# The state matmuls of a linear attention: two heads per matmul, attached to the bursts of the local attention

## Chip, cores, metric

One core of a Trainium2 chip. The metric is device microseconds (us) of one execution. A "drain" below is the time, some 0.1 us, that TensorE loses where the tile size of its matmuls changes.

## The reference, cut to what matters

Two attentions over the same `x` (2048 tokens, 1024 columns, 32 heads of 32) are mixed by a gate. Branch A is linear: a state `kv` (32 x 32 per head) and `z` are summed over all tokens. Branch B is local: every token looks at 8 keys, two apart.

```python
def _A_ref(x, wqkv, wo):
    q, k, v = ...                                   # [B, 32 heads, S, 32]
    phi = lambda t: jnp.where(t > 0, t + 1, jnp.exp(t)) + 1e-6
    pq, pk = phi(q), phi(k)
    kv = jnp.einsum("bhsd,bhse->bhde", pk, v)       # the state
    z = jnp.einsum("bhsd->bhd", pk)
    o = jnp.einsum("bhqd,bhde->bhqe", pq, kv) / (jnp.einsum("bhqd,bhd->bhq", pq, z)[..., None] + 1e-6)
    return o... @ wo
def _B_ref(x, wqkv, wo):
    ...                                             # scores over 8 keys two apart, softmax, times v, @ wo
g = _sigmoid((x * gate_w).sum(-1, keepdims=True))
return g * a + (1 - g) * b
```

## The kernel before

The kernel is written as a list of operations; a planner in it then orders each engine's instructions by costs, dependencies and priorities (`P.op`), and gives an `"any"` operation to ScalarE or VectorE. Any edit can therefore move other operations too. A dense group is 8 pairs of a weight load and a matmul of 128x128 weights with 512 columns. Between the groups stand bursts of small matmuls: the scores S (32 on 64x64 tiles) and the outputs PV (64 on 64x64 tiles) of branch B, run together as S+PV, and the state of branch A for two token tiles at a time, which was a burst of its own:

```python
        def state(two):
            bank = main.next()
            def fn(e):
                for s in range(8):
                    for i, (t, pkt, azt) in enumerate(two):
                        for c in range(4):                                  # 64 pairs, 128x32 tiles, 33 columns
                            h = 16 * (s // 4) + 4 * c + s % 4
                            last = e.matmul(bank.ap()[32*c:32*c+32, s*33:s*33+33], pkt[:, h*32:(h+1)*32], azt[:, h, :],
                                            start=(i == 0), stop=(i == len(two) - 1), tile_position=(0, 32 * c))
            def add(): ...                                                  # kva += bank, 264 columns, VectorE
        def run_state():
            fn, rd, bank, add = state([states.pop(0)[1] for _ in range(2)])
            P.op("pe", fn, 0.55, mode="k", reads=rd, writes=[bank.iv], name="kv")
            add()
        for t in range(NT):                                                 # 16 token tiles, 4 dense groups each
            ...
                slot(1.0 if r == 1 and t % 4 < 3 else 0.0)                  # may start S+PV
                if r == KVAT and t % 2 and t > 1:
                    run_state()
```

`pkt` is phi(k) of a token tile, `azt` its v with a column of ones for z.

```python
        for c in range(4):
            for I in range(2):
                P.op("sp", lambda e, c=c, I=I: e.dma_start(ws[1][...], A_wo[...]), 0.6, writes=[...], prio=40, ...)
```

## Time and profile before

| | before |
|---|---|
| time, median of 3 runs | 484.01 us (483.87 to 484.08) |
| busy: TensorE, VectorE, ScalarE | 472.3, 280.3, 149.3 us |
| state: matmuls, bursts, cost of one burst | 512, 8, 0.71 us |
| first scores, first fold of the state | 129.09, 319.84 us |

Nothing but TensorE's own stream bounds it. The last row marks a stretch that is used as a yardstick: between its ends every kernel has all the scores, outputs and states and exactly 760 dense weight loads. It takes 190.75 us here. Its difference between two kernels is what the bursts and the waits of the stretch make, with some 0.3 us of chance, and without the start and the end of the kernel.

### The profile page before, as it was taken

The page shows a single profiled execution, that of the slowest core. Times are in us where ns is not written, and L with a number is a line of the kernel's source. Part 1 is how long each engine was busy: PE and PEld are TensorE (multiplying, and loading weights), DVE is VectorE, ACT ScalarE, POOL GpSimd, SP SyncE. Part 2 cuts the span into 40 slices and gives each one's busy share as a digit, 9 for nine tenths or more (in the row PEclk, how much of TensorE's full clock was granted, in tenths as well). Part 3 has the DMA queues.
Part 4 walks back from the last instruction along what each step waited for, and adds up shares of the span by engine and source line. Part 5 has one row for each costly group of instructions (what it writes and reads, how often), then busy time and mean ns, then how long its engine had stood idle before and what let it go on. Part 6 is the DMA issues. An engine that isn't in the chain of part 4 may idle for free.

```text
span 482.1 us, 10165 instructions
## 1 busy us (share of the span) xinstructions
PE 472.3 (98%) x4349; PEld 224.3 (47%) x4403; DVE 280.3 (58%) x578; ACT 149.3 (31%) x238; POOL 5.8 (1%) x36
## 2 busy tenths in 40 slices
PE   8999999999999999999999999999999999999997
PEld 3444444444444544545444555444444444444443
DVE  2121435878687788565747565697489136653434
ACT  2111111235333345435434335345532130111000
POOL 4000000000000000000000000000000000000000
DMA  8999992232014359742213414720186019840212
GB/s 225 218 215 311 357 363 46 65 111 87 1 33 141 87 139 203 163 82 69 76 43 83 101 33 99 215 46 1 15 223 156 0 17 235 228 24 2 88 68 90
DMA packets 72951, 57.39 MB, mean 119 GB/s; under 512 B 37953, under 2 KB 60865, under 8 KB 72898
## 3 DMA queue, kind: packets, MB, share of 16 engines
q1 hardware_dynamic: 72210, 56.07, 45.0%
q8 instruction: 36, 0.59, 0.5%
q10 hardware_dynamic: 688, 0.59, 0.4%
q14 instruction: 17, 0.14, 0.1%
HBM read 34.49 MB, written 13.76 MB: 100 GB/s over the span
## 4 chain that ended last, share of the span: by engine, by line
PE 95%; DVE 2%; ACT 1%; issue 1%
PE ps_all L1343 77%; PE ps_all L1729 11%; PE ps_all L1485 2%; PE ps_all L1450 2%; ACT E L1464 1%; PE ps_all L1382 1%; DVE E L1467 1%; DVE pk L1356 1%; PE ps_all L1579 0%; PE ps_all L1674 0%; DVE qd L1440 0%; PE ps_all L1646 0%; DVE e L1354 0%; DVE rs L1501 0%; DVE ot L1502 0%
## 5 line engine op out<-in xcount | busy, mean ns | idle before, releaser
L1343 PE MATMUL ps_all<-w,xT 128*128 128x512 bf16 x930 | 206.9, 380 | 3.7 <-issue 2.5
L1343 PE MATMUL ps_all<-xT,w 128*128 128x512 bf16 x750 | 165.8, 379 | 1.8 <-issue 1.3
L1343 PEld LDWEIGHTS ps_all<-w,xT 128*128 128x128 bf16 x960 | 92.3, 98 | 110.1 <-issue 1.6
L1343 PEld LDWEIGHTS ps_all<-xT,w 128*128 128x128 bf16 x768 | 74.2, 98 | 89.4 <-issue 1.3
L1729 PE MATMUL ps_all<-w,qT 128*128 128x512 bf16 (+1 forms) x260 | 55.4, 372 | 0.2
L1729 PEld LDWEIGHTS ps_all<-w,qT 128*128 128x128 bf16 x264 | 25.9, 98 | 29.6
L1374 DVE CAST vst<-ps_all 128x512 bf16<-128x512 f32 x15 | 10.4, 694 | 43.1 <-PE ps_all L1343 43.1
L1464 ACT ACTIVATE E<-ps_all 128x1824 bf16<-128x1824 f32 (+1 forms) x18 | 30.4, 1687 | 14.1 <-PE ps_all L1485 14.1
L1354 DVE TENSOR_SCALAR e<-e 128x512 bf16<-128x512 bf16 x64 | 18.5, 289 | 27.4 <-ACT e L1352 13.7
L1733 DVE SCALAR_TENSOR_TENSOR o<-ps_all,gm,xT 128x512 bf16<-128x512 f32 (+1 forms) x25 | 18.0, 728 | 21.1 <-PE ps_all L1729 21.0
L1352 ACT ACTIVATE e<-ps_all 128x512 bf16<-128x512 f32 x32 | 19.1, 597 | 34.8 <-PE ps_all L1343 34.8
L1350 ACT ACTIVATE e<-ps_all 128x512 bf16<-128x512 f32 x32 | 19.1, 597 | 27.6 <-PE ps_all L1343 26.5
L1302 DVE TENSOR_TENSOR mx<-mx,kT 128x1024 bf16<-128x1024 bf16 x32 | 21.0, 684 | 9.8 <-ACT kT L1375 9.6
L1502 DVE TENSOR_TENSOR ot<-ps_all,rs 128x480 bf16<-128x480 f32 (+1 forms) x54 | 25.8, 505 | 0.0
L1375 ACT ACTIVATE az<-ps_all 128x512 bf16<-128x512 f32 x24 | 14.4, 599 | 36.2 <-PE ps_all L1343 36.2
L1501 DVE RECIPROCAL rs<-ps_all 128x15 f32<-128x15 f32 (+1 forms) x54 | 9.4, 203 | 27.8 <-PE ps_all L1485 25.9
L1302 DVE TENSOR_TENSOR mx<-mx,qT 128x1024 bf16<-128x1024 bf16 x32 | 21.0, 684 | 6.8 <-ACT qT L1378 6.7
L1375 ACT ACTIVATE vst<-ps_all 128x512 bf16<-128x512 f32 x17 | 10.2, 599 | 47.5 <-PE ps_all L1343 47.5
L1375 ACT ACTIVATE kT<-ps_all 128x512 bf16<-128x512 f32 x21 | 12.5, 596 | 36.0 <-PE ps_all L1343 36.0
L1378 ACT ACTIVATE qT<-ps_all 128x512 bf16<-128x512 f32 x20 | 11.9, 597 | 34.4 <-PE ps_all L1343 34.4
L1356 DVE SCALAR_TENSOR_TENSOR pk<-ps_all,e 128x512 bf16<-128x512 f32 x32 | 21.6, 678 | 0.2
L1378 ACT ACTIVATE xT<-ps_all,g 128x512 bf16<-128x512 f32 x10 | 6.9, 687 | 45.1 <-PE ps_all L1343 45.1
(73 smaller groups left out, 276.8 us busy)
## 6 DMA issues: line engine op xcount, KB each, us to landing
rb<-rc_hbm SPq DMA_DIRECT2D x32, 256.0 KB, 5.9
w<-in_A_wqkv_dram SPq DMA_DIRECT2D x6, 1024.0 KB, 8.8
v<-vB_hbm SPq DMA_DIRECT2D x36, 132.0 KB, 2.9
vB_hbm<-vst SPq DMA_DIRECT2D x32, 132.0 KB, 5.8
w<-in_B_wqkv_dram SPq DMA_DIRECT2D x4, 1024.0 KB, 8.3
xn<-in_A_x_dram SPq DMA_DIRECT2D x16, 256.0 KB, 2.6
out_dram<-o SPq DMA_DIRECT2D x15, 256.0 KB, 2.2
oB_hbm<-ot SPq DMA_DIRECT2D x36, 96.0 KB, 2.2
```

The costliest lines, as they stand in the source:

```text
L1302: P.op("dve", lambda e, m=m, op=op: e.tensor_tensor(m[:, 0:n], m[:, 0:n], src, op), 0.08 + n / 1920.0, reads=[m.all(), reg], writes=[m.all()],
L1343: last = e.matmul(bank.ap(), lhs(dc), rhs(dc), start=(dc == 0), stop=(dc == 7))
L1350: P.op("act", lambda e: e.activation(e_[:, :], bank.ap(), ACT.Exp), act(512), reads=[bank.iv], writes=[e_.all()])
L1352: P.op("act", lambda e: e.activation(e_[:, :], bank.ap(), ACT.Exp, accum_out=qe[:, col:col + 1]), act(512) + 0.1, reads=[bank.iv], writes= ...
L1354: P.op("dve", lambda e: e.tensor_scalar(e_[:, :], e_[:, :], 1.0, 1e-6, op0=ALU.min, op1=ALU.add), 0.25, reads=[e_.all()], writes=[e_.all()])
L1356: P.op("dve", lambda e: e.scalar_tensor_tensor(out=dst, in0=bank.ap(), scalar=0.0, in1=e_[:, :], op0=ALU.max, op1=ALU.add), dps(512), read ...
L1375: fa = lambda e: e.activation(dst, src(), ACT.Copy)
L1378: fa = lambda e: e.activation(dst, src(), ACT.Copy, scale=scale)
L1464: P.op("act", lambda e: e.activation(E[:, 0:32 * nq].rearrange("p (j q) -> p j q", j=4), ps[:, 4:8, 0:8 * nq], ACT.Exp), act(32 * nq), rea ...
L1502: P.op("dve", lambda e, r=r, src=src, dst=dst, m=m: e.tensor_tensor(dst, src()[:, :, 0:32], r[:, 0:m, None].to_broadcast([128, m, 32]), AL ...
L1729: last = e.matmul(bank.ap(0, f1 - f0), qT[:, dc, t * 128:(t + 1) * 128], ws[3][:, dc, f0:f1], start=(dc == 0), stop=(dc == 7))
L1733: P.op("dve", lambda e, bank=bank, o_=o_, t=t, n=n, i0=i0, i1=i1, tgt=tgt, c0=c0: e.scalar_tensor_tensor(out=o_[:, i0 * 128:i1 * 128].rear ...
```

## The change

Its intent: fewer and larger state matmuls (64 weight columns are two heads of phi(k), times two heads of v; the two cross products are computed and never read), and no burst of their own, so that TensorE changes its tile size less often. The accumulator becomes 128 x 528. Seven slots of 66 columns fill one bank; half of the eighth goes to free columns of the first score bank.

```diff
@@ fill (the scores' operand)
-                P.op("any", {"act": fa, "dve": fd}, ...
+                eng = ("act", "dve")[k]
+                P.op(eng, {"act": fa, "dve": fd}[eng], ...
@@ values (outputs)
+                with_state = len(states) > 1 and states[1][0] <= slot_n[0]
                 P.op("pe", each, 1.0 if s_fn else 0.55, mode="c", ..., name="S+PV" if s_fn else "PV")
+                add = run_state() if with_state else None      # its addition is placed after the outputs are moved out
@@ state
-                        for c in range(4):
-                            h = 16 * (s // 4) + 4 * c + s % 4
-                            last = e.matmul(bank.ap()[32 * c:32 * c + 32, s * 33:s * 33 + 33], pkt[:, h * 32:(h + 1) * 32], azt[:, h, :], ...
-                                            tile_position=(0, 32 * c))
+                        for k in range(2):
+                            h = 16 * (s // 4) + 8 * (s // 2 % 2) + 4 * k + 2 * (s % 2)
+                            lhs = pkt[:, 32 * h:32 * h + 64]
+                            if s < 7:
+                                outs_ = [(bank.ap(66 * s, 66 * s + 66), azt[:, h:h + 2, :])]
+                            else:
+                                outs_ = [(bank.ap(462, 495), azt[:, h, :]), (SO[0].ap(456, 489), azt[:, h + 1, :])]
+                            for o, rhs in outs_:
+                                last = e.matmul(o[64 * k:64 * k + 64, :], lhs, rhs, ..., tile_position=(0, 64 * k))
@@ add: 264 columns become 495 (bank) and 33 (SO[0])
@@ run_state
-            P.op("pe", fn, 0.55, mode="k", reads=rd, writes=[bank.iv], name="kv")
-            add()
+            P.op("pe", fn, 0.5, mode="c", reads=rd, writes=[bank.iv, SO[0].iv], name="kv")
+            return add
@@ token tiles
-                if r == KVAT and t % 2 and t > 1:
-                    run_state()
@@ totals: one copy kva -> kvb becomes eight of 32 rows x 128 columns, on ScalarE or VectorE
```

More of the change, by code (lines that the diff above doesn't have):

```diff
@@ L1192, in build_kernel @@
     zsel = SB([128, 8, 32], BF16, "zsel")
-    kva = SB([128, 8, 33], F32, "kva")
+    kva = SB([128, 528], F32, "kva")
     mx4 = SB([128, 4], F32, "mx4")
@@ L1231, in build_kernel @@
     MASKLAG = 12
-    KVAT = 1
     WARM = 11
@@ L1441, in fill @@
                 fa = lambda e, k=k: e.activation(Q[:, :, k, 0:2 * nq], src, ACT.Copy, scale=par[:, k:k + 1])
-                P.op("any", {"act": fa, "dve": fd}, {"act": act(16 * nq), "dve": 0.15 + 16 * nq / 1920.0}, reads=[qT.part((0, 8), (t0 + qs, t0 + qs + 2 * nq)), par.all()],
+                eng = ("act", "dve")[k]
+                P.op(eng, {"act": fa, "dve": fd}[eng], {"act": act(16 * nq), "dve": 0.15 + 16 * nq / 1920.0}[eng], reads=[qT.part((0, 8), (t0 + qs, t0 + qs + 2 * nq)), par.all()],
                      writes=[Q.part((0, 8), (k, k + 1), (0, 114))], after=held)
@@ L1487, in each, with evacuate @@
                     return last
+                with_state = len(states) > 1 and states[1][0] <= slot_n[0]
                 P.op("pe", each, 1.0 if s_fn else 0.55, mode="c", reads=[vt.all(), E.all()] + list(s_reads), writes=[b.iv for b in SO + two], name="S+PV" if s_fn else "PV")
-                return (lambda: evacuate(two)) if s_fn is not None else evacuate(two)
-            def evacuate(two):
+                add = run_state() if with_state else None
+                return (lambda: evacuate(two, add)) if s_fn is not None else evacuate(two, add)
+            def evacuate(two, add):
                 o, os_ = ot.next()
@@ L1503, in evacuate @@
                          reads=reads + [r.all()], writes=[reg])
+                if add is not None:
+                    add()
                 last_evac.append(P.ops[-1])
@@ L1576, in fn @@
                     for i, (t, pkt, azt) in enumerate(two):
-                        for c in range(4):
-                            h = 16 * (s // 4) + 4 * c + s % 4
-                            last = e.matmul(bank.ap()[32 * c:32 * c + 32, s * 33:s * 33 + 33], pkt[:, h * 32:(h + 1) * 32], azt[:, h, :],
-                                            start=(i == 0), stop=(i == len(two) - 1), tile_position=(0, 32 * c))
+                        for k in range(2):
[6 more added lines that the diff above has]
+                            for o, rhs in outs_:
+                                last = e.matmul(o[64 * k:64 * k + 64, :], lhs, rhs, start=(i == 0), stop=(i == len(two) - 1), tile_position=(0, 64 * k))
                 return last
             def add():
-                src = lambda: bank.ap(0, 264).rearrange("p (i c) -> p i c", c=33)
-                if two[0][0] == 0:
-                    P.op("dve", lambda e: e.tensor_copy(kva[:, :, :], src()), dps(264), reads=[bank.iv], writes=[kva.all()])
-                else:
-                    P.op("dve", lambda e: e.tensor_tensor(kva[:, :, :], src(), kva[:, :, :], ALU.add), dps(264), reads=[bank.iv, kva.all()], writes=[kva.all()])
+                for lo, n, b in ((0, 495, bank), (495, 33, SO[0])):
+                    c = 0 if b is bank else 456
+                    src = b.ap(c, c + n)
+                    dst, reg = kva[:, lo:lo + n], kva.part((lo, lo + n))
+                    if two[0][0] == 0:
+                        P.op("dve", lambda e, dst=dst, src=src: e.tensor_copy(dst, src), dps(n), reads=[b.iv], writes=[reg])
+                    else:
+                        P.op("dve", lambda e, dst=dst, src=src: e.tensor_tensor(dst, src, dst, ALU.add), dps(n), reads=[b.iv, reg], writes=[reg])
             return fn, [x.all() for _, p, a in two for x in (p, a)], bank, add
@@ L1614, in plan @@
                 slot(1.0 if r == 1 and t % 4 < 3 else 0.0)
-                if r == KVAT and t % 2 and t > 1:
-                    run_state()
         assert not todo
         def last_state():
-            run_state()
+            run_state()()
             totals()
@@ L1629, in totals @@
         def totals():
-            P.op("dve", lambda e: e.tensor_reduce(mx4[:, 3:4], kva[:, :, 32:33], AX.XY, ALU.max), 0.2, reads=[kva.all()], writes=[mx4.part((3, 4))], prio=1e5)
-            P.op("dve", lambda e: e.tensor_copy(kvb[:, :, :], kva[:, :, 0:32]), 0.35, reads=[kva.all()], writes=[kvb.all()])
-            P.op("dve", lambda e: e.transpose(kvT[:, :], kvb[:, :, :].rearrange("p s d -> p (s d)")), 0.4, reads=[kvb.all()], writes=[kvT.all()])
+            kv4 = kva[:, :].rearrange("p (s c) -> p s c", c=66)
+            P.op("dve", lambda e: e.tensor_reduce(mx4[:, 3:4], kv4[:, :, 32:33], AX.XY, ALU.max), 0.2, reads=[kva.all()], writes=[mx4.part((3, 4))], prio=1e5)
+            for c in range(4):
+                for a in range(2):
+                    k = 2 * (c % 2) + a
+                    src = kva[32 * k:32 * k + 32, :].rearrange("p (i j q f) -> p i j q f", i=2, j=2, q=2)[:, :, c // 2, :, 33 * a:33 * a + 32]
+                    dst = kvb[32 * c:32 * c + 32, :, :].rearrange("p (i q a) d -> p i q a d", i=2, q=2)[:, :, :, a, :]
+                    fd = lambda e, dst=dst, src=src: e.tensor_copy(dst, src)
+                    fa = lambda e, dst=dst, src=src: e.activation(dst, src, ACT.Copy)
+                    P.op("any", {"act": fa, "dve": fd}, {"act": 0.3, "dve": 0.27}, reads=[kva.all()], writes=[[("K", 2 * c + a, 2 * c + a + 1, None)]])
+            P.op("dve", lambda e: e.transpose(kvT[:, :], kvb[:, :, :].rearrange("p s d -> p (s d)")), 0.4, reads=[[("K", 0, 8, None)]], writes=[kvT.all()])
             for c in range(4):
@@ L1635, in totals @@
                     k = 4 * (c % 2) + r
-                    P.op("dve", lambda e, c=c, r=r, k=k: e.tensor_copy(zsel[32 * r:32 * r + 32, c:8:4, k:k + 1], kva[32 * c:32 * c + 32, r:8:4, 32:33]), 0.16,
+                    P.op("dve", lambda e, c=c, r=r, k=k: e.tensor_copy(zsel[32 * r:32 * r + 32, c:8:4, k:k + 1], kv4[64 * (c % 2) + 32 * (r % 2):64 * (c % 2) + 32 * (r % 2) + 32, 2 * (c // 2) + r // 2:8:4, 32:33]), 0.16,
                          reads=[kva.all()], writes=[zsel.all()], prio=1000 + len(P.ops) + 100)
```

## The prediction

> **What bounds the kernel now.** I read the page's totals first, then the chain that ended last, then TensorE's waits in the stretch that holds the state bursts, and last the order of time around a few bursts.
>
> From the page, busy time by engine, and the chain's shares by engine:
> ```profile
> PE 472.3 (98%) x4349; PEld 224.3 (47%) x4403; DVE 280.3 (58%) x578; ACT 149.3 (31%) x238; POOL 5.8 (1%) x36
> ...
> PE 95%; DVE 2%; ACT 1%; issue 1%
> ```
> TensorE (PE) is busy 98% of 482.1 us and carries 95% of the chain. VectorE and ScalarE have much room, so a change pays only by what it takes from TensorE. The waits of TensorE between 200 and 330 us (total us, times, longest):
> ```profile
> PE ps_all L1343 <- issue: 2.5, 16, 0.2
> PE ps_all L1343 <- DVE pk L1356: 0.6, 4, 0.2
> ```
> All twenty are the same 0.16 us after a burst of small matmuls. Even these look like a lost record: the order of time shows 15 or 31 matmuls where whole groups of 8 make 16 or 32, and the weight load of the missing one starts 0.22 us earlier. So TensorE waits for nobody there, and the four waits for `pk` last no longer than the others. The order of time on TensorE (start, length, line, shape, count):
> ```profile
> 260.00 6.85 PE L1343 MATMUL ps_all<-w,xT 128*128 128x512 bf16 x31 [0.16 <-issue]
> 266.79 0.60 PE L1450 MATMUL ps_all<-qd,kT 64*64 64x114 bf16 x32
> 267.22 0.67 PE L1485 MATMUL ps_all<-v,E 64*57 64x33 bf16 x64
> 268.05 3.40 PE L1343 MATMUL ps_all<-w,xT 128*128 128x512 bf16 x15 [0.16 <-issue]
> 271.38 0.67 PE L1579 MATMUL ps_all<-az,pk 128*32 128x33 bf16 x64
> 272.21 10.31 PE L1343 MATMUL ps_all<-w,xT 128*128 128x512 bf16 x47 [0.16 <-issue]
> ...
> 304.73 3.40 PE L1343 MATMUL ps_all<-w,xT 128*128 128x512 bf16 x15 [0.16 <-issue]
> 308.06 0.68 PE L1485 MATMUL ps_all<-v,E 64*56 64x33 bf16 x64
> 308.90 3.40 PE L1343 MATMUL ps_all<-xT,w 128*128 128x512 bf16 x15 [0.16 <-issue]
> ```
> L1450 is the scores, L1485 the outputs, L1579 the state. Spacing of the dense matmuls: (6.85 - 0.379)/30 = 0.2157 us, 3.451 us for 16. A burst costs the distance between the dense starts around it less the dense work: state 272.21 - 268.05 - 3.451 = **0.71 us**, outputs alone 308.90 - 304.73 - 3.451 = 0.72, scores and outputs joined 268.05 - 260.00 - 6.902 = 1.15. The eight state bursts together are 8 x 0.71 = 5.7 us, 1.2% of the span. That is the most that could ever be won.
>
> Inside one state burst: the dense stream before it ends at 268.05 + 15 x 0.2157 = 271.29, the first small matmul starts at 271.38, so the change of tile size costs 0.09 us going in. The last small one starts at 271.38 + 0.67 - 0.184 = 271.87, so the body is 0.49 us, 7.7 ns for each of 63 pairs of load and matmul. The next dense one (the lost record, 272.21 - 0.216) is at 271.99: 0.12 us going out, 0.11 after the last one has streamed. Scores to outputs, both on 64x64 tiles, costs nothing: outputs start 0.43 us after the scores, which is 32 x 13.4 ns.
>
> **What the Trainium skill says.** "TensorEngine Tiling (Array Packing)", Key Properties: "Changing tiling mode (not just tile) drains the TensorE". The trace agrees, with about 0.1 us for each change. The denominators, 128x32 tiles with 512 columns, show it too:
> ```profile
> 342.88 0.60 PE L1674 MATMUL ps_all<-xT,zsel 128*32 128x512 bf16 x8
> 343.42 0.39 PE L1343 MATMUL ps_all<-xT,w 128*128 128x512 bf16 x1
> ```
> The last starts at 342.88 + 0.60 - 0.379 = 343.10 and has streamed at 343.32; the dense one follows 0.10 us later.
>
> "TensorE: Matmul & The Clock Gate", Part 3, The mechanism, gives about 4 ns between starts on different tiles. 7.7 ns for a load and a matmul is twice 3.9, so it agrees: the old burst is bound by its number of instructions, not by columns. Its four tiles would stream 64 x 33 columns in 64 x 33/4 x 0.417 = 220 ns.
>
> The same page, "LDWEIGHTS (loading the stationary operand)", puts a load at columns/1.2 ns: 53 ns for 64 columns. The trace does not agree. Loads by shape (busy us, mean ns):
> ```profile
> L1485 PEld LDWEIGHTS ps_all<-v,E 64*57 64x57 bf16 x1024 | 10.2, 103 | 0.0
> L1450 PEld LDWEIGHTS ps_all<-qd,kT 64*64 64x64 bf16 x576 | 8.1, 105 | 7.6 <-issue 7.2 <-DVE mx L1766 0.4
> L1579 PEld LDWEIGHTS ps_all<-az,pk 128*32 128x32 bf16 x512 | 4.5, 93 | 3.4 <-DVE e L1354 2.5 <-issue 0.4 <-DVE ot L1502 0.4
> ```
> From 32 to 64 columns the duration grows by 12 ns, 0.38 ns a column, and 57-column loads keep pace with 7.7 ns a pair on four tiles, at most 31 ns per load and tile. So I take 64 x 0.42 = 27 ns for one load.
>
> "PSUM — Partial Sum Buffer", PSUM bank collisions, says two engines must not be in one bank and quadrant together even at other columns. So the part of the new state that lies in the first score bank (columns 456 to 488) makes the exponential wait for the state burst; no run here shows a collision.
>
> **The change part by part.**
>
> *Matmuls.* 64 pairs of 32x33 become 36 per burst: 7 slots x 2 tiles x 2 column halves = 28 of 66 columns, and 8 of 33 for the split last slot. Only two 64-column tiles run at once. On one tile the next pair can start after max(66 x 0.417 + 2.5 = 30, load 27) = 30 ns, so 15 ns a pair: 28 x 15 = 420 ns, and 8 x 13.5 (load-bound) = 108. Body **0.53 us against 0.49**: half the products are thrown away, and the burst turns from bound by instructions to bound by the array. Nearly half the instructions gone gains nothing by itself: +0.04 us.
>
> *Attaching.* By the slots in the code, S+PV runs at the last group of tiles 1, 4, 5, 8, 9, 12 and 13 with two states waiting: 7 of 8 states are attached, the last stands alone as before. Each attached one loses its own going in and out, 0.21 us. But it goes from 64x64 to 128x64 tiles, which is another tile size; by the drain rule that costs 0.1 again. Net -0.11 + 0.04 = -0.07 us.
>
> *Sum on TensorE.* 7 x -0.07 + 1 x 0.04 = **-0.45 us**.
>
> *VectorE.* One addition of 264 elements (0.42 us in the trace) becomes 495 and 33: at about 1.04 ns an element on 0.14 us fixed, 0.66 + 0.17. 8 x 0.41 = +3.3 us. Eight of the 26 `qd` products (0.449 us) move to ScalarE (1.046 us): -3.6 and +8.4 us. With 58% and 31% busy, these are beside TensorE's work.
>
> *Waits that move.* The exponential starts some 0.65 us later. In the tightest place its mask ends at 230.35 and the outputs that need it start at 234.75, 4.4 us of slack. The end of the state (eight small copies on two engines in place of one of 0.29 us, then the transpose) takes about 1 us longer; the transpose ended at 314.75 and its first user, the fold, starts at 319.84. None reaches TensorE.
>
> **The rivals.**
>
> 1. *The change 64x64 to 128x64 costs nothing* (the column width stays). Then 7 x (-0.21 + 0.04) + 0.04 = -1.15 us: 482.9. For it: scores to outputs are free. Against: every change of tile size in the trace costs about 0.1. A quarter.
> 2. *The loads don't hide under the matmuls of their own tile, or cost 53 ns.* Then a pair takes (27 + 30)/2 = 28 ns, or 27 by the load alone, the body is 0.9 to 1.0 us, and 8 x 0.4 to 0.5 = 3.2 to 4 us are added, less 0.77: about 487. Against: eight loads of the denominators are issued from 342.44 within 0.12 us, while the first four 512-column matmuls hold all four tiles. One in ten.
> 3. *TensorE waits.* For tiles 1, 5, 9 and 13 the state needs the `az` of the group just before S+PV. At tile 5 that copy runs from 226.28 to 226.88, and S+PV ends at 227.37: 0.5 us to spare. If ScalarE were held up, up to 0.3 us four times, 484.7. And joined bursts take three of the four free banks at once; the next group takes the bank of the `az` copy, done by then, and the one after that comes 1.7 us later, when the first output bank has been emptied. I expect no wait. The planner also reorders all engines anew, which may add or take some tenths.
>
> **Range and chances.** 484.01 - 0.45 = 483.56, rounded to **483.5**. The lower end is rival 1 plus luck in the plan (482.4). The upper holds small waits and a partly load-bound burst (485.2), not all of rival 2. Faster by 2% would need 9.7 us, and all state bursts are only 5.7: 0.01. Slower by 2% would need a failed plan with long waits: 0.02. Within 2%: 0.97.
>
> **What would show it.** State matmuls 288 in place of 512, about 15 ns apart, body 0.50 to 0.56 us; seven directly after an output burst with about 0.1 us between the last output's start and the first state's, one alone. Dense-to-dense distance around a joined burst less its dense work: about 1.15 + 0.64 = 1.79 us. No wait of TensorE over 0.2 us in that stretch. The prediction is wrong if the body is 0.8 us or more (loads), if the gap is missing (rival 1), or if TensorE waits for `az`, `kva` or a bank after a joined burst.

## The result, and the profile after

The changed kernel took 484.15 us (483.45 to 484.79, 6 runs), the kernel before 483.95 (483.80 to 484.24, 6 runs): ratio 1.0005, interval 0.9992 to 1.0018. That is the same time, inside the predicted range. But the 0.45 us that the working expected to win are not there, and that is what has to be explained.

The profiled run was the slowest of the six (484.79). The page's totals and the chain by engine:

```profile
PE 472.4 (98%) x4129; PEld 224.9 (47%) x4179; DVE 286.3 (59%) x587; ACT 154.5 (32%) x244; POOL 5.8 (1%) x36
...
PE 93%; DMA 3%; SPq 1%; issue 1%; DVE 0%
```

220 TensorE matmuls fewer (288 in place of 512 for the state, and a few records that are missing from one trace or the other), and the same busy time. DMA has come into the chain of waits with 3% (most of it is the whole duration of two loads of `v`, 7.3 and 4.6 us, through which the chain now runs back; the wait itself is 0.6 us). TensorE's waits from 180 to 330 us (total us, times, longest) say where:

```profile
PE ps_all L1342 <- issue: 2.2, 14, 0.2
PE ps_all L1450 <- DMA v<-vB_hbm: 0.6, 1, 0.6
```

The first row is the lost record after a burst that the prediction read in the old trace (the traces of r1, r2, r3 and r4 below lost none, and there the row or its 0.16 us pieces are gone). The second is new. The order of time on TensorE shows its place, and an undisturbed joined burst (start, length, line, shape, count):

```profile
188.89 5.13 PE L1342 MATMUL ps_all<-w,xT 128*128 128x512 bf16 x23 [0.16 <-issue]
194.62 0.60 PE L1450 MATMUL ps_all<-qd,kT 64*64 64x114 bf16 x32 [0.60 <-DMA v<-vB_hbm]
...
218.77 0.67 PE L1485 MATMUL ps_all<-v,E 64*56 64x33 bf16 x64
219.37 0.75 PE L1589 MATMUL ps_all<-az,pk 128*64 128x66 bf16 x36
220.27 6.85 PE L1342 MATMUL ps_all<-w,xT 128*128 128x512 bf16 x31 [0.16 <-issue]
```

The same place in the kernel before:

```profile
188.52 6.85 PE L1343 MATMUL ps_all<-w,xT 128*128 128x512 bf16 x31 [0.16 <-issue]
195.30 0.60 PE L1450 MATMUL ps_all<-qd,kT 64*64 64x114 bf16 x32
```

Three things are to be seen. Before, 32 dense matmuls (31 and the lost one) stood ahead of this S+PV and it started at 195.30 without a wait. Now the planner puts 24 there, the stream is ready at 194.0, and it waits 0.60 us for the load of `v`. The load itself is no later than it was: by the DMA view its last part was issued at 189.40 and landed 4.5 us later in the kernel before (193.9; 194.4 in r11), and at 189.90 and 4.6 us later in the changed one (194.5; 193.9 in r1). The kernel before had 0.8 to 1.4 us to spare there, and starting 8 matmuls (1.7 us) sooner used up more than that. In the joined burst the last output starts at 218.77 + 0.67 - 0.18 = 219.26 and the first state at 219.37: the gap of 0.11 us that the prediction put there for the change of tile size. And the state's starts spread over 0.75 - 0.183 = 0.57 us for 35 steps: 16.2 ns a pair, where 15 was predicted. The groups of the state (busy us, mean ns of one):

```profile
L1589 PEld LDWEIGHTS ps_all<-az,pk 128*64 128x64 bf16 x288 | 5.2, 111 | 0.6 <-issue 0.4
L1589 PE MATMUL ps_all<-az,pk 128*64 128x66 bf16 x224 | 5.1, 197 | 0.0
```

The other engines did what was worked out: the additions cost 0.664 and 0.174 us (0.66 and 0.17 predicted), the scores' operand is made 18 times by each engine at 0.452 and 1.046 us, the transposed state is ready at 315.5 us and the fold starts at 320.75. ScalarE's exponential now waits for the state burst, seven times; VectorE waits for it in turn, at most 0.3 us a time, and TensorE does not.

The yardstick stretch took 191.29 us in this trace, 190.75 before.

### The profile page after: what moved, and what is told of

It is laid out like the page before. It is cut to its first block, busy times and chain, and to the rows that moved or that the text cites. A ratio compares the mean times of both kernels' runs of the same rounds, so it can differ in the third digit from the quotient of the medians.

```text
span 483.1 us, 9739 instructions
## 1 busy us (share of the span) xinstructions
PE 472.4 (98%) x4129; PEld 224.9 (47%) x4179; DVE 286.3 (59%) x587; ACT 154.5 (32%) x244; POOL 5.8 (1%) x36
## 4 chain that ended last, share of the span: by engine, by line
PE 93%; DMA 3%; SPq 1%; issue 1%; DVE 0%
PE ps_all L1342 77%; PE ps_all L1747 11%; DMA v<-vB_hbm 2%; PE ps_all L1450 2%; PE ps_all L1485 2%; PE ps_all L1589 1%; DMA xT<-in_A_x_dram 1%; SPq L1565 1%; PE ps_all L1692 0%; PE ps_all L1664 0%; SPq L1321 0%; SPq L1316 0%; SPq L1516 0%; DVE az L1373 0%; DVE o L1751 0%
## 5 line engine op out<-in xcount | busy, mean ns | idle before, releaser
L1374 ACT ACTIVATE kT<-ps_all 128x512 bf16<-128x512 f32 x21 | 12.5, 597 | 36.0 <-PE ps_all L1342 36.0
L1373 DVE CAST az<-ps_all 128x512 bf16<-128x512 f32 x15 | 10.4, 694 | 16.3 <-PE ps_all L1342 16.0
L1406 DVE SCALAR_TENSOR_TENSOR xn<-xn,gwb 128x1024 bf16<-128x1024 bf16 x16 | 19.3, 1220 | 1.1 <-DMA xn<-in_A_x_dram 1.1
```

The lines of the kernel that those rows point to most:

```text
L1373: fd = lambda e: e.tensor_copy(dst, src())
L1374: fa = lambda e: e.activation(dst, src(), ACT.Copy)
L1406: P.op("dve", lambda e, t=t, xt=xt: e.scalar_tensor_tensor(out=xt[:, :], in0=xt[:, :], scalar=1.0, in1=gwb[:, :], op0=ALU.mult, op1=ALU.mu ...
```

## The experiments

**My theory**: the joined burst is cheaper than the two bursts apart by one drain, as predicted; the heavier state (bound by its weight loads, at 16 ns a pair) gives nearly all of it back; and the new wait for `v`, which the planner's new order causes while the transfers are congested, takes the rest. **The rival**: the wait and the differences of some tenths are chance of single runs, and the size of the tiles does not matter, so that attaching wins its 0.2 us a burst and something else eats it. **A second question** is why the shape was changed at all: by the measured bursts, the old shape attached should be the better half of the change, and the two-head shape only a loss.

The first four ran on one chip, beside 11 runs of the kernel before with a median of 483.91.

### r1: the changed kernel again

No edit.

> The changed kernel as it is, a second look. In its first trace a joined burst cost 1.83 us beyond the dense work, the lone state 0.78, and TensorE waited 0.60 us for the v load at the second burst of the key/value stage. Theory A (the bursts save about 0.03 us each, 0.15 us in all, and the earlier burst that meets the v load takes 0.6 back): the wait is there again, 0.3 to 0.9 us, and the ratio is 1.000 to 1.0015. Theory B (that wait and the slow start were accidents of one run): no wait over 0.2 us, ratio 0.9990 to 0.9998.

484.24 us (483.91 to 484.40), ratio 1.0007 (0.9994 to 1.0020). The wait is there again, in the order of time on TensorE:

```profile
188.18 5.35 PE L1342 MATMUL ps_all<-w,xT 128*128 128x512 bf16 x24
194.02 0.60 PE L1450 MATMUL ps_all<-qd,kT 64*64 64x114 bf16 x32 [0.49 <-DMA v<-vB_hbm]
...
203.78 13.99 PE L1342 MATMUL ps_all<-w,xT 128*128 128x512 bf16 x64
...
218.73 0.75 PE L1589 MATMUL ps_all<-az,pk 128*64 128x66 bf16 x36
219.41 7.08 PE L1342 MATMUL ps_all<-w,xT 128*128 128x512 bf16 x32
```

This trace lost no matmul here, so the joined burst can be measured cleanly: 219.41 - 203.78 - 64 x 0.2157 = **1.825 us**. Apart, S+PV and the old state cost 1.147 + 0.71 = 1.857. So an attached state wins 0.03 us, not 0.07. The stretch took 190.94. The wait is not chance (r2, r8 and r9, which have the same 24 matmuls there, show it too, with 0.52, 0.3 and 0.51 us).

### r2: attach only, in the old shape

The kernel before, with the state attached and its 64 matmuls of one head unchanged:

```diff
+                with_state = len(states) > 1 and states[1][0] <= slot_n[0]
                 P.op("pe", each, ..., name="S+PV" if s_fn else "PV")
+                add = run_state() if with_state else None
...
-                if r == KVAT and t % 2 and t > 1:
-                    run_state()
```

> Only the attaching: the state keeps its 64 pairs of 32 columns on four tiles, the products of two engines stay free to the planner. TensorE's order is that of the changed kernel, 24 dense matmuls ahead of the second burst included. Drain theory: joined burst 1.15 + 0.11 gap + 0.49 body = 1.75 us (against 1.83 changed), gap between last output and first state matmul 0.10 to 0.12; total 0.5 us under the changed kernel. Theory that the change of shape is what pays: joined burst 1.83 or more. The v wait is there as in the changed kernel.

488.31 us (486.78 to 489.12), ratio 1.0083 (1.0068 to 1.0099): 4.4 us slower, far outside what was expected. The burst itself behaved: 222.25 - 206.70 - 13.805 = 1.745 us, one drain below the 1.857 of the two apart, and the wait for `v` was there as expected (0.52 us). But TensorE stopped twice in the middle of a dense group, with no wait that the profile names:

```profile
195.66 0.67 PE L1583 MATMUL ps_all<-az,pk 128*32 128x33 bf16 x64
196.26 1.47 PE L1343 MATMUL ps_all<-w,xT 128*128 128x512 bf16 x6
199.97 5.77 PE L1343 MATMUL ps_all<-w,xT 128*128 128x512 bf16 x26 [2.24 <-issue]
...
206.70 13.99 PE L1343 MATMUL ps_all<-w,xT 128*128 128x512 bf16 x64
...
222.25 7.08 PE L1343 MATMUL ps_all<-w,xT 128*128 128x512 bf16 x32
...
254.68 0.82 PE L1343 MATMUL ps_all<-w,xT 128*128 128x512 bf16 x3
256.68 6.42 PE L1343 MATMUL ps_all<-w,xT 128*128 128x512 bf16 x29 [1.18 <-issue]
```

Between the two stops lie 893 matmuls with their loads, 1786 instructions. That is 7 x 256 = 1792 but for the six waits of its sequencer, which are instructions too. The Trainium skill, "Runtime: NRT & Kernel Launch", Instruction fetch mechanics, says that an engine's instruction memory is refilled in blocks of 16 KiB, 256 instructions. The trace agrees on the block: the page counts 36 packets and 0.59 MB on the instruction queue q8, 16.4 KB each. And in each stop such a packet is fetched: the first starts in the 0.1 us from 197.4, in the middle of saturated transfers, the second in the 0.1 us from 254.0. The DMA view, which counts a packet where it starts, of the first of them:

```profile
q1 hardware_dynamic: 44, 0.03, 106.2%
q8 instruction: 1, 0.02, 66.8%
```

66.8% of 16 engines in 0.1 us are 1.07 us for this packet (1.24 for the second). TensorE goes on 2.5 and 2.65 us after they start, which is 1.4 us after their end both times. My reading: dense work needs 256 instructions in 128 x 0.2157 = 27.6 us, but the joined burst in the old shape is 160 pairs, 320 instructions, in some 1.6 us; where it swallows a whole block, the next one is not there in time. The burst of the kernel before is 96 pairs (192 instructions), that of the changed kernel 132 pairs (264). This would answer the second question: fewer instructions are the point of the two-head shape. r5, r7 and r10 test the reading. The stops account for the time: the stretch took 194.68 us, 3.9 to 4.2 above the kernel before.

### r3: the new shape alone

The changed kernel with the state back in bursts of its own at the old places, and the operand of the scores again on either engine.

```diff
-                add = run_state() if with_state else None
...
+                if r == 1 and t % 2 and t > 1:
+                    run_state()
```

> Only the new shape: 36 pairs of 64 columns, at the old places by themselves. From the lone state of the changed kernel: 0.78 us each against 0.71 before, 8 x 0.07 = +0.6 us, ratio 1.0008 to 1.0016, no v wait because the second burst has 32 dense matmuls ahead of it again. If fewer instructions paid: 0.6 us or less each and a ratio below 0.9985.

485.31 us (484.32 to 485.79), ratio 1.0024 (1.0011 to 1.0036). A lone burst in the order of time:

```profile
205.37 3.63 PE L1342 MATMUL ps_all<-w,xT 128*128 128x512 bf16 x16
208.92 0.75 PE L1584 MATMUL ps_all<-az,pk 128*64 128x66 bf16 x36
209.60 6.65 PE L1342 MATMUL ps_all<-w,xT 128*128 128x512 bf16 x30
```

209.60 - 205.37 - 3.451 = **0.78 us** against 0.71, so 8 x 0.07 = 0.6 us. The yardstick agrees: 191.38 us, 0.6 to 0.9 above the two traces of before. The ratio is higher than expected, and the rest of it lies ahead of the stretch: the first scores of the profiled run start at 130.01 us in place of 129.09. There is no wait for `v` here.

### r4: the loads of A_wo later

The changed kernel with the eight loads of `A_wo` issued in the middle of the stage (at the sixth token tile, without their priority) in place of just before it.

```diff
-        for c in range(4):                      # ahead of the stage, prio=40
-            for I in range(2): ... e.dma_start(ws[1][...], A_wo[...])
+            if t == 5:                          # in the loop over token tiles, no priority
+                for c in range(4):
+                    for I in range(2): ... e.dma_start(ws[1][...], A_wo[...])
```

> The changed kernel with the eight loads of the output weights of A moved from the busy stretch at 178 to 194 us to tile 5; TensorE's order is the same. If the v load is late because it shares the DMA engines with these loads: the wait goes from 0.6 to under 0.2 us and the time falls by 0.3 to 0.7 us against the changed kernel, ratio about 0.9990 to the kernel before. If v is late for another cause (its own buffer, the queue's order): the wait stays at 0.6.

483.81 us (483.66 to 484.33), ratio 0.9997 (0.9984 to 1.0010), 0.43 us under r1 by the medians (0.30 by the means, with runs that overlap, so the time alone does not show a gain). TensorE has no wait at all between 180 and 330 us, although the same 24 dense matmuls stand ahead of that S+PV:

```profile
189.01 5.35 PE L1342 MATMUL ps_all<-w,xT 128*128 128x512 bf16 x24
194.31 0.60 PE L1450 MATMUL ps_all<-qd,kT 64*64 64x114 bf16 x32
```

Here `v` has landed at 191.75. So the cause of the wait is both: an order that comes 8 matmuls sooner, and transfers that hold `v` up as they did before. The stretch took 190.48 us; the working from the measured bursts is 190.48 to 190.75 (before), less 7 x 0.03, plus 0.07: 190.34 to 190.61. Against the kernel before, r4 can't be told apart.

### r5, r6, r7: move the block boundaries

If the stops of r2 come from block boundaries, instructions added at the very start of TensorE's stream must move them. These three are r2 with other warm-up matmuls (11 wide ones before): 9 wide and 58 tiny ones, 112 instructions more (r5); the same with the late loads of r4 (r6); 9 wide and 42 tiny ones, 80 more (r7), which should put the boundaries inside state bursts. They ran on a second chip with r8, beside 11 runs of before with a median of 484.23.

```diff
-    WARM = 11
+    WARM = 9
+        for i in range(58):                     # 42 in r7
+            P.op("pe", lambda e, i=i: e.matmul(banks[7].ap(0, 33)[32*(i%4):32*(i%4)+32, :], warm[:, 0:32], warm[:, 0:33], ..., tile_position=(0, 32*(i%4))), ...)
```

> The old-shape attached kernel of the run before, with 9 wide and 58 tiny warm-up matmuls in place of 11 wide ones: 112 instructions more ahead of the rest of TensorE's stream, nothing else. In the run before TensorE stood 2.24 and 1.18 us in the middle of dense groups, 893 matmuls and 6 extra waits apart: 1792 instructions, 7 times 256, as if it ran out of instructions at 256-instruction blocks. Fetch theory: a block becomes usable some 3.5 us after the block before it is entered, so a burst of 320 instructions starves TensorE only where both borders fall in or right behind it; with 112 more, no border pair does: no stop over 0.4 us but the v load's (0.5), time 3 us or more under the run before, ratio to the kernel before 0.9985 to 1.001. Rival (the stops come from a bank, a semaphore or the DMA traffic at that place): they stay where they were, 2.2 and 1.2 us, ratio about 1.008.

r5: 491.66 us (486.92 to 493.80), ratio 1.0129 (1.0088 to 1.0169). The stops after the first and fourth joined burst are gone and small ones (0.20, 0.41, 0.56 us) stand elsewhere, so the places moved, and the stretch took 191.55 us, 3.1 less than in r2. The whole time did not follow, because of something else, far behind this stage:

```profile
429.45 20.20 PE L1343 MATMUL ps_all<-w,xT 128*128 128x512 bf16 x78 [3.71 <-DVE o L1738]
```

TensorE stood still for 3.71 us, waiting for a bank that VectorE couldn't empty, because an output write took up to 12.5 us to land; and after this the same 78 matmuls took 20.20 us in place of 78 x 0.2157 = 16.8. The trace shows why: the granted clock is 0.53 from 428 to 432 us and 0.62 from 432 to 436, and 1.00 on both sides. The mean clock of four of the six runs was 0.992 to 0.997; the two with 1.0 took 486.92 and 488.06 us, still more than was expected.

> The same with the output weights of A loaded at tile 5, so that the v load is in time. If drain, fetch and v load are all that matters: joined burst 1.745 to 1.755 us, no stop over 0.4 us, 7 x 0.11 = 0.77 us under the kernel before, ratio 0.998 to 0.9992. If something else of the change costs time: ratio 1.000 or more.

r6: 490.35 us (489.13 to 491.63), ratio 1.0121 (1.0104 to 1.0139). The same far stop, 3.41 us, here costs 5.3 us with the slow matmuls after it (clock 0.58 from 428 to 432 us), and the first scores start 1.24 us late. The stretch itself was as good as that of r4, 190.64 us: attaching in the old shape is no better even where its worst stops are away, as small ones of 0.2 to 0.3 us remain (one state burst took 0.93 us) and eat what its cheaper bursts win. It was meant as a version that beats both, and it did not.

> The old-shape attached kernel with 80 instructions more (9 wide, 42 tiny warm-ups). Fetch theory: the stops move to two other bursts, some 2.2 us each: near the end of the state matmuls of the burst of tile 4 (about 222 us) and of tile 13 (about 297 us); none at 197 to 200 and 255 to 257 us. Rival: the stops stay at 197 to 200 and 255 to 257 us.

r7 (one look): 503.87 us at a mean clock of 0.986. Its state bursts in the order of time:

```profile
198.26 0.45 PE L1586 MATMUL ps_all<-az,pk 128*32 128x33 bf16 x34 [3.30 <-issue]
...
226.87 0.20 PE L1586 MATMUL ps_all<-az,pk 128*32 128x33 bf16 x3 [1.83 <-issue]
...
302.51 0.23 PE L1586 MATMUL ps_all<-az,pk 128*32 128x33 bf16 x8 [2.29 <-issue]
```

The second and third are where the theory put them, inside the state bursts, after 61 and 56 of their 64 matmuls. The first was not expected. The stops of this trace are 7.4 us in all, and after the first and the third the clock falls again (0.53 from 197 to 204 us, 0.57 from 303 to 307); its stretch took 202.25 us.

A count in the kept traces settles the cause. Number all instructions of TensorE in a trace (two for each pair, and the waits of its sequencer): r2, r5, r6, r7 and r10 have thirteen stops of over 0.19 us in or just behind a joined burst (lost records aside), and TensorE goes on from every one of them at an instruction whose number leaves the same remainder by 256, namely 192, whatever the shift, and 1.3 to 1.6 us after the end of a packet of instructions. So in these stops TensorE stands at a block boundary and waits for the next block. When a block arrives, above all while transfers are saturated, I can't predict well. What held up the output writes of r5, r6 and r7 (4.59 us in r7) is not settled. It belongs to these three kernels, the only ones with the tiny warm-ups: they need 167.8 to 169.2 us from the first fold to the end, r8 on the same chip 162.2 and all others 162.2 to 162.6.

### r8: the state on tiles of the size of the outputs

The changed kernel, wrong (relative error 0.06): each state matmul uses the first 64 tokens only, so its tiles are 64x64 like those of the outputs.

```diff
-                            lhs = pkt[:, 32 * h:32 * h + 64]
+                            lhs = pkt[0:64, 32 * h:32 * h + 64]
-                                outs_ = [(bank.ap(66 * s, 66 * s + 66), azt[:, h:h + 2, :])]
+                                outs_ = [(bank.ap(66 * s, 66 * s + 66), azt[0:64, h:h + 2, :])]
```

> Wrong result on purpose: the changed kernel, but the state uses the first 64 tokens of each tile only, so its matmuls stand on 64x64 tiles as scores and outputs do; 36 pairs, 66 columns, all else the same. Drain theory: no gap between the last output and the first state matmul (start to start under 0.03 us in place of 0.11), the joined burst falls by about 0.1 to 1.73 us, the lone state stays at 0.78. If the gap is a change of operands or of burst and not of tile size: it stays at 0.1, joined burst 1.83.

484.12 us (one look). The gap is gone:

```profile
204.56 13.76 PE L1342 MATMUL ps_all<-w,xT 128*128 128x512 bf16 x62 [0.16 <-issue]
...
218.69 0.67 PE L1485 MATMUL ps_all<-v,E 64*56 64x33 bf16 x64
219.19 0.74 PE L1589 MATMUL ps_all<-az,pk 64*64 64x66 bf16 x36
220.08 6.85 PE L1342 MATMUL ps_all<-w,xT 128*128 128x512 bf16 x31 [0.16 <-issue]
```

The last output starts at 218.69 + 0.67 - 0.18 = 219.18, the first state 0.01 us later. The joined burst is 220.08 - 204.56 - 13.805 = 1.715 us against 1.825 (the first record after the burst is lost on both sides, so the distance stands). The change from 64x64 to 128x64 tiles costs 0.11 us. (So in four of the seven joined bursts. In the other three, at 227, 260 and 292 us, 0.07 us are left, and there an instruction of TensorE's sequencer, the wait for the copy of `az`, stands between outputs and state.) That part of the rival, and with it the prediction's own first rival, falls.

### r9: half the columns

The changed kernel, wrong: every state matmul moves 33 columns in place of 66. If the burst is bound by columns it must shrink; if by loads, it must not.

```diff
-                                outs_ = [(bank.ap(66 * s, 66 * s + 66), azt[:, h:h + 2, :])]
+                                outs_ = [(bank.ap(66 * s, 66 * s + 33), azt[:, h, :])]
```

> Wrong result on purpose: the changed kernel with 33 moving columns in every state matmul in place of 66; loads, tiles and count (36 pairs) the same. The body in the changed kernel is 0.57 us, 16.2 ns a pair, where I had reckoned 15. If the load of 64 columns onto its own tile sets the pace (some 32 ns): the body stays at 0.53 to 0.57 us, 15 to 16 ns a pair. If the streaming of 66 columns does (27.5 ns and a fixed part): it falls to 0.45 us or less, under 13 ns a pair.

485.52 us (one look, on a third chip beside r10 and r11, with a median of before of 483.96):

```profile
220.15 0.75 PE L1589 MATMUL ps_all<-az,pk 128*64 128x33 bf16 x36
221.06 6.85 PE L1342 MATMUL ps_all<-w,xT 128*128 128x512 bf16 x31 [0.16 <-issue]
```

Still 0.75 us for 36, so the columns that are moved do not set the pace. What is left is the load of its tile, or a fixed price of a pair. The single starts in the traces speak for the load: with 33 columns moved each time, a tile takes a pair every 25 ns with a load of 32 columns (the first 32 pairs of the old state burst), every 28 to 30 ns with 57 columns (the first 32 pairs of an output burst) and every 32 ns with 64 columns (here). With half the rows loaded (r8) it stays at 32. After its first 32 pairs the old burst goes on at 8.5 ns a pair; its 7.7 ns are the mean of the two parts (6.3 and 8.5). The total is no measure of the shape: two output bursts of this trace ran 0.3 and 0.5 us long (at 188 and 204 us), and the wait for `v` was 0.51.

### r10: another shift, late loads, and r11: the kernel before

r10 is r2 with 3 warm-ups in place of 11 (16 instructions fewer) and the late loads; 3 rounds. r11 is the kernel before, for its trace.

```diff
-    WARM = 11
+    WARM = 3
```

> Old shape attached, output weights of A later, and 3 warm-up matmuls in place of 11: 16 instructions fewer ahead of everything. Fetch theory: the stop in the burst of tile 1 (2.2 us) shrinks to about 0.6 or less and the one of tile 8 (1.2 us) to nothing, because each block now lasts 8 dense matmuls longer; perhaps 0.2 us at tile 5. Fewer warm-ups may cost some tenths at the start. Time about 484 to 485, 3.5 us or more under the first old-shape attached kernel. Rival (the stops belong to the place): 2.2 and 1.2 us again, about 488.

485.49 us (485.01 to 486.02), ratio 1.0025 (1.0008 to 1.0042). The two stops of r2 are gone, and two others, of 0.5 and 0.8 us, stand inside state bursts. With the first scores 1.4 us late besides (130.50), it is 2.8 us under r2 and still above before. One of the two stops was not where I expected it.

> The kernel before once more, for a second trace: state burst 0.71 us, scores and outputs joined 1.15, no wait for v. If the differences in the start (first scores at 129.1 before, 129.0 to 130.3 in the others) are chance, it may be anywhere there; if the changed kernels' starts are slower, 129.1 again.

483.73 us; first scores at 129.03, the stretch 190.48, no wait for `v`. So the wait belongs to the changed order, not to a later `v` (194.4 us here).

## Why the prediction was right, and where it was not

Right for the reason given: the state is 1.2% of the span and on a stream that nothing else bounds, so no shape of it can move the time by 2%.

**Attaching removes a drain on each side and puts one back: right.** The gap is 0.11 us (r1 and after), 0.01 with equal tiles (r8), and the old shape attached costs 1.745 in place of 1.857 (r2): 0.11 each, as the sum had it.

**Seven attached, one alone, 288 matmuls: right.**

**The body, "0.53 us against 0.49": mis-sized.** It is 0.57 us. The failed term is "So I take 64 x 0.42 = 27 ns for one load": on its tile a pair comes every 32 ns, with 66 columns or 33 (r9). It was drawn from how the duration of a load grows with its columns, and that isn't its spacing. The better number was one sentence earlier in the prediction: 57-column loads at "at most 31 ns per load and tile" was hardly an upper bound to be undercut: those loads come every 28 to 30 ns. (The 0.417 ns a column and the 2.5 ns of the prediction's sum, whose source it does not give, are borne out by the spacings in these traces: 215.7 ns for 512 columns, 50.8 ns on one tile for the 114 of the scores. They did not bind.) "Bound by its number of instructions" was half right for the old burst: its first 32 pairs are bound by their tiles, the rest comes at 8.5 ns a pair. With 0.08 in place of 0.04 a state the sum is 7 x (-0.11 + 0.08) + 0.08, and as measured 7 x -0.03 + 0.07 = **-0.14 us** in place of -0.45.

**"None reaches TensorE", "I expect no wait": wrong.** A wait of 0.49 to 0.60 us for `v` takes the 0.14 back and 0.4 more. I had read TensorE's waits from 200 us on, where the old state bursts were; the new plan attaches the first state at 195.6, in a place where the order changed and the transfers were saturated. The old trace had the landing of `v`, at 193.9 us, 1.4 us ahead of the S+PV at 195.30; that this S+PV would come 8 matmuls (1.7 us) sooner only the new plan says. The third rival named the planner with "some tenths" but not the place. The sum is now -0.14 + 0.5 to 0.6 = +0.35 to +0.45 us, against +0.2 and +0.3 measured between medians and +0.2 to +0.8 in the yardstick stretch (191.29 and 190.94 against 190.75 and 190.48). Without the wait (r4) it is -0.1 between medians and 0.0 to -0.3 in the stretch, which fits the sum, though too small to be told from nothing in time.

**VectorE, ScalarE: right in each size, wrong in one split.** The planner gave VectorE 7 more of the `az` copies too, so VectorE rose by 6.0 us and ScalarE by 5.2, not by about 0 and 8. TensorE waits for neither.

**The rivals.** The first (no drain) falls by r8. The second (a body of 0.9 us) falls by 0.57. The third came in another form.

**What stays open.** The first scores start between 128.9 and 130.5 us in these kernels, and between 128.97 and 129.46 in two runs of the changed one; a part of every comparison below 1 us is this, and I did not find what it hangs on. That TensorE stops at instruction blocks is shown by the count after r7; how long before a block is asked for, and so which burst starves, is not understood. What pauses single output bursts (0.05 to 0.5 us, in most traces) is not known either; those of r2 (at 188 us) and r8 (at 204) do not lie at a block boundary. The joined burst of the changed kernel, 264 instructions, is itself a little over one block. All its runs here have the same boundaries, so that it never stops for a block was seen for one placing only; whether another would cost it time is not tested.

## What to carry to other kernels

Where small matmuls on disjoint tiles follow each other, the price of a pair here was the largest of three: the rate at which instructions follow, as I read it (8.3 to 8.5 ns a pair after the first 32 of a burst; not tested), the columns that its own tile moves (51 ns for 114), and the load of its own tile (25 to 32 ns for 32 to 64 columns). Fewer tiles at once make the last two dearer. Take the load from the spacing of a burst of the same width, not from the durations. Before a planned order is changed, look at the waits at the places where work will newly stand, with the transfers of that time, not at those where it stood. And joining bursts saves a drain only as long as the burst does not use up TensorE's instructions faster than they are fetched: the attachment cost 4.4 us with 320 instructions in a burst (1.5 us with other boundaries and late loads, r10) and about nothing with 264, placed as they were.

## What the Trainium skill lacked or had wrong

- "TensorE: Matmul & The Clock Gate", LDWEIGHTS (loading the stationary operand): columns/1.2 ns would be 53 ns for 64 columns. On two tiles the pairs follow each other at 32 ns on each tile, whether 66 or 33 columns are moved after each load (r9), so a load there takes no longer than that.
- "TensorEngine Tiling (Array Packing)", Key Properties: it states the drain at a change of tiling mode, without its size. Here it is 0.09 to 0.12 us each time, and 0.01 between tiles of the same size (r8).
- "Runtime: NRT & Kernel Launch", Instruction fetch mechanics: the cost of crossing a block is called mostly hidden. In a burst of 320 instructions it was not: stops of 1.2 to 3.3 us (r2, r7), the engine going on 1.4 us after the end of the packet (r2). The page gives TensorE 2048 instructions in one sentence and only two blocks in another; the stops are hard to explain with eight blocks ahead, and would fit two: the first stop of r2, after 3264 instructions (12.75 blocks), ends with the 12th packet of the trace.
- No page gives the smallest spacing of a pair of load and matmul on four tiles: in the old burst 6.3 ns for the first 32 pairs and 8.5 ns for the rest.
